# Weight sums for the output products: added by VectorE out of SBUF, and all weight sums begun earlier on a timer of their own

## The chip, the core and the metric

The kernel runs as one program on one NeuronCore of a Trainium2 chip. The metric is the device time of one execution in microseconds. A core has a matrix engine (TensorE, PE in the profile; its weight loads are PEld), a vector engine (VectorE, DVE), a scalar engine (ScalarE, ACT), a general engine (GpSimd, POOL) and a sync engine (SyncE, SP) whose queue issues most transfers. PE writes its results to PSUM; DVE and ACT take them from there to SBUF. All engines run at once and wait for each other through semaphores.

## The reference

Attention over four batches, eight heads, 768 positions of 64, in which each query sees the 31 nearest keys and 24 block summaries (the maximum over each block of 32 keys, the mean over each block of 32 values); then a gated network:

```python
def _moe_ref(x, w1, w2, w3, w_out):      # x: 3072 x 512, the heads side by side
    a = x @ w1                           # 512 x 1024
    b = x @ w2                           # 512 x 1024
    h = a * b @ w3                       # 1024 x 1024
    return (h @ w_out)                   # 1024 x 512
```

All inputs and outputs are float32. Since nothing stands between the last two products, the kernel multiplies `w3 @ w_out` once (1024 x 512) and uses that as the one output weight.

## The kernel before

**Products.** A float32 matrix is held as two halves of a narrower type, a high one and the rest ("low", `low` at L120), and a product takes three matmuls: high by high, low by high, high by low. Nearly every matmul of the network is 128 x 128 by 128 x 512. I count work in such matmuls and call one a *product* (512 columns; `U` in the code is 512, and the counter `given` counts columns handed to PE).

**Stages.** The 3072 tokens are six blocks of 512. PE's order is fixed by the program (a manual schedule for PE), as one stream (`products_in_order`, L973): 192 products that fold `w3 @ w_out` into the eight tiles `wp[0..7]` (each 128 x 2 x 512: high and low); then blocks 0 and 1 in the plain way (`gate`, `project`: 192 + 96 products for each block); then blocks 2+3 and blocks 4+5 in pairs (`gates`, `project_fast`) by a scheme with seven block products for eight (`NK = 7`), with 336 + 168 products for each pair. So the first pair begins at product 192 + 2 x 288 = 768. In between, `run` (L996) cuts the stream and the attention work of a pair of heads is put in (`two_steps`, L1282): scores (`sc`), softmax, transposes (`tp`), outputs (`po`).

**Weight sums.** The seven-product scheme needs sums of weight blocks. For the gates they are made per quarter q = 0..3 (`sums_of_gates`, L936), for the output weights per half c = 0, 1 (`sums_of_output`, L947). Both use `stationary` (L664), a generator. It loads four blocks `a11, a12, a21, a22` of 128 x 512 into a tile `wr`; four DVE instructions (L689, L691, L695, L700) make the four sums; for each sum `finished` makes a high half on ACT (L679) and a low half on DVE (L121) in a tile `sp`, and SP stores `sp` to DRAM (L685; `wS` for gates, `pS` for the output). The products load them again from there through `flow_in` (L712), at most six tiles `ws` ahead, and only sums whose store is in the set `stored`. Products that need no sum come from spilled weights (`spill_weights`, `spill_wp`).

For a gate quarter the load is four DVE additions of high and low halves out of SBUF (L942). For an output half it is a way through DRAM: `spill_high` (L927) stores the high half of each `wp[i]` into a tile `pR`; `join_wp` (L930) adds the low half onto it by an accumulating transfer that POOL issues; `load` (L949) then fetches four pieces of 256 KB into `wr` from SP, and waits nine steps.

**Pace.** The sums are a list `background` of generators, the moving operands of the pairs (`moving_x`, L766) a list `tasks`. `tend` (L981) takes one step of the first task, or, where no task can go on, one step of the first sum; `run` calls it every 4.5 products (`4.5 * U`), and whenever the stream cannot go on. The four gate sums enter the list in slot 64 of the first part (L1176), the output sums in the attention steps (8,1) and (9,0) (L1262). The slots from 47 to 66 share the stream evenly up to `TO_SLOTS` (437 products).

**Order on the queues.** PE is always in program order. SP is in program order in the first part (up to 437 products), POOL in the second. Elsewhere a planner orders ACT, DVE and SP: an instruction that comes earlier in the program goes first among those that the planner holds to be ready by its own cost estimates. On the chip each engine works its queue strictly in the planned order, so an instruction that waits holds everything behind it.

**Buffers.** Tag `x` has six buffers: the four `x` tiles of a plain block, the gate sums' `sp` tiles and all `ws` tiles. Tag `ring` has five (raw weights, pairs of `h`, gate sums' `wr`, later `hr`). Tag `wp` has eight (the `wp` tiles, later `tmp` and the output sums' `sp`). Tag `raw` has two (keys and values of later batches, the output sums' `wr`).

Of the kernel before, what the change touches and what calls it, by code (L numbers as in the profile page):

```python
# [11 lines left out]
F32 = mybir.dt.float32  # L12
# [4 lines left out]
ALU = mybir.AluOpType  # L17
# [3 lines left out]
P = 128  # L21
# [32 lines left out]
RING = 5  # L54
# [19 lines left out]
def attention_moe(ctx, tc, qG, kW, kT, vP, vW, vB, mask, w1, w2, w3T, wo, out, outT):  # L74
    nc = tc.nc
    B, NPAIR, _, S = kT.shape
    S -= PAD
    NB = S // BLOCK
    U = TOKENS
# [10 lines left out]
    NF = w1.shape[0] * FQ // P  # L90
    NJ = w3T.shape[2] // 2 // P
    DO = out.shape[1]
    NK = 7
# [19 lines left out]

    wS = [[tc.dram_tile([P, 2, KH * FQ], F32, name=f"wS{k}_{q}") for q in range(NQ)] for k in range(NK)]
    pS = {k: [tc.dram_tile([P, 2, 2 * DH], F32, name=f"pS{k}_{c}") for c in range(NF // 4)] for k in range(2, NK - 1)}
    pR = [tc.dram_tile([P, 2, 2, DO], F32, name=f"pR{c}") for c in range(NF // 4)]
    pW = [tc.dram_tile([P, 2, DO], F32, name=f"pW{i}") for i in range(NF)]
    vS = [tc.dram_tile([P, P], F32, name=f"vS{b}") for b in range(B)]

# [533 lines left out]
    def staggered(works):  # L653

        active = []
        while works or active:
            if works:
                active.append(works.pop(0))
            active = [work for work in active if next(work, 0)]
            yield 1  # L660

    stored = set()

    def stationary(name, load, to_dram, home, apart=False):  # L664


        if apart:
            two = [sb.tile([P, 2, 512], F32, name="wr", tag="raw", bufs=2) for _ in range(2)]
            t = [[two[i][:, j] for j in range(2)] for i in range(2)]
        else:  # L670
            whole = sb.tile([P, 2, 2, 512], F32, name="wr", tag="ring", bufs=RING)
            t = [[whole[:, i, j] for j in range(2)] for i in range(2)]
        yield from load(t)
        (a11, a12), (a21, a22) = t
        yield 1

        def finished(k, raw):
            to = sb.tile([P, 2, 512], F32R, name="sp", **home)
            nc.scalar.copy(to[:, 0], raw)  # L679
            yield 1  # L680
            low(nc.vector, to[:, 1], raw, to[:, 0])
            yield 1
            yield 1
            yield 1
            nc.sync.dma_start(to_dram(k), to.bitcast(F32))  # L685
            stored.add((name, k))

        works = []
        nc.vector.tensor_tensor(a22, a21, a22, ALU.add)  # L689
        yield 1  # L690
        nc.vector.tensor_tensor(a21, a11, a21, ALU.subtract)  # L691
        works.append(finished(2, a22))
        next(works[0])
        yield 1
        nc.vector.tensor_tensor(a11, a22, a11, ALU.subtract)  # L695
        works.append(finished(5, a21))
        next(works[0])
        next(works[1])
        yield 1
        nc.vector.tensor_tensor(a12, a12, a11, ALU.subtract)  # L700
        if apart:
            yield from staggered([*works, finished(4, a11), finished(3, a12)])
            return

        yield from staggered(works)
        for _ in range(3):
            yield 1
        yield from staggered([finished(4, a11), finished(3, a12)])

# [56 lines left out]
    def moving_x(n, at):  # L766

        o = ORDERS[n]
        k = o.ids[at]

        def start():
            while any(kept.get((n, half), 0) < NC for half in range(2 if k > 1 else 1)):
                yield -1
            t = sb.tile([P, 2, KH, U], F32R, name="xT", tag="w12", bufs=8)
            works = []
            for c in range(KH):
                b = [[raws[n, half][c + i * KH] if (n, half) in raws else None for half in range(2)] for i in range(2)]
                works.append(moving(o, k, b, (t[:, 0, c], t[:, 1, c]), o.before.get(k, (k,))))
            yield from staggered(works)
            xT[n, k] = t  # L780

        tasks.append(start())
# [141 lines left out]
        n = DO if i >= NF // 2 else DH  # L924
        nc.sync.dma_start(pW[i][:, :, :n], wp[i][:, :, :n].bitcast(F32))

    def spill_high(i):  # L927
        nc.sync.dma_start(pR[i % (NF // 2) // 2][:, i // (NF // 2), i % 2], wp[i][:, 0].bitcast(F32))

    def join_wp(i):  # L930


        to = pR[i % (NF // 2) // 2][:, i // (NF // 2), i % 2]
        nc.gpsimd.dma_start(to, wp[i][:, 1].bitcast(F32), accum_op=ALU.add)

    def sums_of_gates(q):  # L936

        def load(t):
            for j, w in enumerate(("w1", "w2")):
                hi, lo = (weights[w, q][:, i].rearrange("p (k c) f -> p k (c f)", k=2).bitcast(F32) for i in range(2))  # L940
                for c in range(2):
                    nc.vector.tensor_tensor(t[j][c], hi[:, c], lo[:, c], ALU.add)  # L942
                yield 1

        return stationary("w%d" % q, load, lambda k: wS[k][q], {"tag": "x", "bufs": 6})

    def sums_of_output(c):  # L947

        def load(t):  # L949
            for h in range(2):  # L950
                for i in range(2):
                    to = t[i][h].rearrange("p (j d) -> p j d", d=DH)
                    nc.sync.dma_start(to, pR[c][:, h, :, i * DH : (i + 1) * DH])
            yield from range(1, 10)

        return stationary("p%d" % c, load, lambda k: pS[k][c], {"tag": "wp", "bufs": NF}, True)

    def network():
        for u in range(2):
# [16 lines left out]
        yield from network()  # L976

    stream = products_in_order()
    given, tended = [0.0], [0.0]

    def tend():  # L981


        some = False
        for works in (tasks, background):
            while works:
                n = next(works[0], 0)
                if n > 0:
                    return True
                if n < 0:  # L990
                    break
                works.pop(0)
                some = True
        return some

    def run(columns):  # L996

        while given[0] < columns:
            n = next(stream, 0)
            if n <= 0:  # L1000
                if n == 0 or not tend():
                    return
                continue
            given[0] += n
            if given[0] >= tended[0]:
                tended[0] = max(tended[0] + 4.5 * U, given[0])
                tend()

    def place(s):
        return divmod(s, NPAIR)  # L1010
# [162 lines left out]
        66: [lambda: fetch_sums(6)],  # L1173
        67: [lambda: fetch_sums(7)],
    }
    WORK.setdefault(64, []).append(lambda: background.extend(sums_of_gates(q) for q in range(NQ)))  # L1176
    for q in range(NQ):
        WORK.setdefault(46 + 3 * q, []).append(lambda q=q: spill_weights(q))
    for i in range(NF):
        WORK.setdefault(48 + i, []).append(lambda i=i: spill_wp(i))  # L1180
    for i in range(NF):
        WORK.setdefault(58 + i, []).append(lambda i=i: spill_high(i))
    RATE = 8000
    LATER_RATE = 2744

# [65 lines left out]
    def begins(m):  # L1251
# [7 lines left out]
    EXTRA = {  # L1259
        (7, 0): [lambda: moving_x(1, 0), lambda: moving_x(1, 1)],  # L1260
        (8, 0): [lambda: gates_flow(1), lambda: flow_in(4), lambda: moving_x(1, 2)],
        (8, 1): [lambda: background.append(sums_of_output(0))],  # L1262
        (9, 0): [*(lambda k=k: moving_x(1, k) for k in range(3, NK)), lambda: background.append(sums_of_output(1))],
    }
    for i in range(NF):
        EXTRA.setdefault((4 + i // 4, i // 2 % 2), []).append(lambda i=i: join_wp(i))

    turned = {}

# [140 lines left out]
```

## Time and profile before

| | |
|---|---|
| median of 3 runs | 518.35 us (513.8 to 519.22) |
| the profiled execution | 515.73 us |
| its span, first to last instruction | 513.9 us |
| mean granted PE clock | 0.99 |
| matmuls of the network that take most: `ln` of the gates | 672, 155.3 us busy |
| output sums: first and last fetch of `pR` | 241.1 and 322.5 us |
| output sums: first and last store to `pS` | 312.5 and 344.8 us |
| first and last fetch of `pS` as `ws` | 352.9 and 488.5 us |

The profiled execution spends 515.73 - 513.9 = 1.83 us outside its span. PE's busy time is a union of overlapping matmuls, so the idle time of PE, and stretches in which the same matmuls take longer, are what can be gained or lost.

### The profile page before, as it was taken

The numbers are of one execution on the slowest core, as the hardware profiler recorded it, in microseconds if no ns is written. First come the engines' busy times: TensorE is split into PE (matmuls) and PEld (weight loads), VectorE is DVE, ScalarE is ACT, GpSimd is POOL, SyncE is SP. The second block draws the span as 40 slices with busy tenths as digits, with TensorE's granted clock in tenths as the row PEclk, the third lists the DMA queues.
The fourth block names the chain that finished last, engine by engine and source line by source line (L and its number), as shares of the span: only waits on it lengthen the run. The fifth ranks groups of instructions, "written<-read, shape, count | busy, mean of one in ns | idle before, by whom it ended". The sixth has DMA issues, their size and how long they took to land.

```text
span 513.9 us, 10576 instructions
## 1 busy us (share of the span) xinstructions
PE 484.7 (94%) x3804; PEld 395.2 (77%) x3804; DVE 363.5 (71%) x881; ACT 313.6 (61%) x874; POOL 92.6 (18%) x177
## 2 busy tenths in 40 slices
PE   0889999999998969999889999999999999999997
PEld 0667778888877858888678888878888888888886
DVE  5969886897768588697176597469999029229972
ACT  5489864775889569686399487853734421522710
POOL 1024522100435242335040402020000000000000
PEclk9999999999999979999989999999999999999999
DMA  8998698999799999899876698997669766556652
GB/s 346 412 408 264 228 352 280 370 399 411 245 296 265 318 270 289 274 293 318 277 203 220 206 347 298 329 300 245 206 190 282 230 198 204 186 185 204 208 187 98
DMA packets 53764, 139.29 MB, mean 271 GB/s; under 512 B 6224, under 2 KB 19280, under 8 KB 51152
## 3 DMA queue, kind: packets, MB, share of 16 engines
q1 hardware_dynamic: 45072, 111.78, 63.3%
q0 software_dynamic: 7488, 24.75, 16.9%
q10 hardware_dynamic: 1152, 2.10, 1.2%
q8 instruction: 30, 0.49, 0.4%
q14 instruction: 22, 0.18, 0.1%
HBM read 105.89 MB, written 32.70 MB: 270 GB/s over the span
## 4 chain that ended last, share of the span: by engine, by line
PE 71%; ACT 10%; DMA 9%; DVE 7%; issue 1%; SPq 1%; ACTq 0%; DVEq 0%
PE ln L740 42%; PE mm L125 21%; DMA wS<-sp 3%; DMA v<-vS 3%; PE po L457 3%; ACT sm L404 3%; PE sc L376 3%; DVE wf L206 2%; DVE w L121 2%; PE tp L434 2%; DMA wr<-pR 1%; ACT w L220 1%; ACT sm L414 1%; DVE wf L203 1%; DMA wraw<-in_wo_dram 1%
## 5 line engine op out<-in xcount | busy, mean ns | idle before, releaser
L740 PE MATMUL ln<-xT,ws 128*128 128x512 f32 x672 | 155.3, 391 | 1.0 <-DVE hr L760 1.0
L740 PEld LDWEIGHTS ln<-xT,ws 128*128 128x128 f32 x672 | 125.4, 188 | 28.3 <-DVE hr L760 1.4
L125 PE MATMUL mm<-x,w 128*128 128x512 f32 x384 | 90.6, 396 | 0.0
L125 PEld LDWEIGHTS mm<-x,w 128*128 128x128 f32 x384 | 72.8, 191 | 16.2 <-issue 0.5
L404 ACT ACTIVATE sm<-sm,mx 128x120 f32<-128x120 f32 x192 | 73.6, 390 | 9.0 <-DVE mx L390 9.0
L740 PE MATMUL ln<-hT,ws 128*128 128x512 f32 (+1 forms) x348 | 76.9, 382 | 0.0
L760 DVE TENSOR_TENSOR tmp<-ln,tmp 128x512 f32<-128x512 f32 (+1 forms) x53 | 35.8, 677 | 57.2 <-PE ln L740 43.0
L740 PEld LDWEIGHTS ln<-hT,ws 128*128 128x128 f32 x348 | 63.8, 188 | 12.7
L125 PE MATMUL mm<-w,w 128*128 128x512 f32 x192 | 50.0, 410 | 14.8 <-ACT w L220 12.2
L642 ACT CAST hT<-hr 128x512 fp32r<-128x512 f32 x56 | 32.2, 622 | 50.7 <-DVE hr L817 40.1
L125 PEld LDWEIGHTS mm<-w,w 128*128 128x128 f32 x192 | 36.0, 193 | 25.7 <-ACT w L220 12.9
L414 ACT ACTIVATE sm<-sm,mx 128x120 f32<-128x120 f32 x128 | 40.3, 388 | 10.5 <-DVE mx L410 6.4
L125 PE MATMUL mm<-wp,h 128*128 128x512 f32 x192 | 46.3, 395 | 0.0
L390 DVE CUSTOM_DVE_ANT_0 sm<-sc,mask_sb 128x120 f32<-128x120 f32 x192 | 40.7, 276 | 6.2 <-PE sc L376 6.2
L125 PEld LDWEIGHTS mm<-wp,h 128*128 128x128 f32 x192 | 35.4, 188 | 8.4 <-issue 0.5
L325 POOL DMA_DIRECT2D v<-in_vW_dram x48 | 25.3, 565 | 72.8 <-PE po L457 66.9
L121 DVE TENSOR_TENSOR hT<-hr,hT 128x512 fp32r<-128x512 f32 x56 | 35.5, 685 | 3.5 <-ACT hT L642 3.3
L404 ACT ACTIVATION_READ_ACCUMULATOR sm<-sm,mx 128x1 f32 x192 | 37.3, 194 | 0.0
L376 PE MATMUL sc<-k,q 64*64 64x120 f32 x768 | 26.6, 274 | 5.4 <-issue 3.9
L121 DVE TENSOR_TENSOR w<-wf,w 128x1024 fp32r<-128x1024 f32 (+1 forms) x22 | 25.6, 1166 | 8.2 <-ACT w L220 8.2
L220 ACT CAST w<-wf 128x1024 fp32r<-128x1024 f32 (+1 forms) x22 | 21.4, 973 | 14.8 <-DVE wf L206 13.4
L758 ACT COPY tmp<-ln 128x512 f32<-128x512 f32 x32 | 18.6, 586 | 16.8 <-PE ln L740 15.5
(74 smaller groups left out, 588.4 us busy)
## 6 DMA issues: line engine op xcount, KB each, us to landing
ws<-wS SPq DMA_DIRECT2D x56, 512.0 KB
wraw<-in_w3T_dram SPq DMA_DIRECT2D x8, 1024.0 KB
wraw<-in_w_dram SPq DMA_DIRECT2D x8, 1024.0 KB
wS<-sp SPq DMA_DIRECT2D x16, 512.0 KB
ws<-pS SPq DMA_DIRECT2D x16, 512.0 KB
wS<-w SPq DMA_DIRECT2D x12, 512.0 KB
ws<-pW SPq DMA_DIRECT2D x24, 256.0 KB
k<-in_kW_dram POOLq DMA_DIRECT2D x14, 368.0 KB, 8.4
```

Of the source, the lines that this page charges most:

```text
L121: eng.tensor_tensor(dst, src, hi.bitcast(F32), ALU.subtract)
L125: nc.tensor.matmul(acc, lhsT=a, rhs=b, start=first and i == 0, stop=last and i == len(terms) - 1)
L220: nc.scalar.copy(t[:, 0, some], f[:, some])
L325: (nc.gpsimd if u > 1 else nc.sync).dma_start(v[rows, g], vW[u, p, rows, g])
L376: nc.tensor.matmul(sc[h][64 * g : 64 * g + 64, i * KR : (i + 1) * KR], lhsT=q[rows, i * P + 64 * g : i * P + 64 * g + 64], rhs=k[rows, i, ...
L390: nc.vector.tensor_tensor_reduce(out=sm[:, j], in0=sc[h][:, i * KR : (i + 1) * KR], in1=mask_sb[:, 0 if blk == 0 else 2 if blk == BLOCKS - ...
L404: nc.scalar.activation(sm[:, j], sm[:, j], AF.Exp, bias=mx[:, 0, j : j + 1], scale=-1.0, accum_out=mx[:, 1, j : j + 1])
L414: nc.scalar.activation(sm[:, j], sm[:, j], AF.Copy, scale=mx[:, 2, j : j + 1])
L642: nc.scalar.copy(dst[0], src)
L740: nc.tensor.matmul(bank[:, cols], lhsT=x, rhs=y[:, cols], start=c + j == 0 and (split or k in o.first), stop=c == steps - 1 and j == 2 and ...
L758: nc.scalar.copy(parts[to][:, cols], got)
L760: nc.vector.tensor_tensor(parts[to][:, cols], got, parts[more][:, cols], ALU.add)
```

## The change

The way through DRAM is taken out: the tiles `pR`, `spill_high`, `join_wp` and their slots are gone. The load of an output sum becomes eight DVE additions of 128 x 256, straight from the high and low halves in `wp`, two to a step. Its `wr` now comes from tag `ring` and its `sp` tiles from tag `x`, as for the gates, and the `apart` variant is gone. All six sums enter the list in slot 58, gates first. Sums have a timer of their own (every 3.3 products) and no longer wait until no task can go on; the tasks keep the timer of 4.5. In every sum two more steps lie between the first two stores and the second two (5 for 3).

```diff
-    pR = [tc.dram_tile([P, 2, 2, DO], F32, name=f"pR{c}") for c in range(NF // 4)]
...
-    def stationary(name, load, to_dram, home, apart=False):
-        if apart:
-            two = [sb.tile([P, 2, 512], F32, name="wr", tag="raw", bufs=2) for _ in range(2)]
-            t = [[two[i][:, j] for j in range(2)] for i in range(2)]
-        else:
-            whole = sb.tile([P, 2, 2, 512], F32, name="wr", tag="ring", bufs=RING)
-            t = [[whole[:, i, j] for j in range(2)] for i in range(2)]
+    def stationary(name, load, to_dram, home):
+        whole = sb.tile([P, 2, 2, 512], F32, name="wr", tag="ring", bufs=RING)
+        t = [[whole[:, i, j] for j in range(2)] for i in range(2)]
...
-        if apart:
-            yield from staggered([*works, finished(4, a11), finished(3, a12)])
-            return
         yield from staggered(works)
-        for _ in range(3):
+        for _ in range(5):
             yield 1
         yield from staggered([finished(4, a11), finished(3, a12)])
...
-    def spill_high(i):
-        nc.sync.dma_start(pR[i % (NF // 2) // 2][:, i // (NF // 2), i % 2], wp[i][:, 0].bitcast(F32))
-    def join_wp(i):
-        to = pR[i % (NF // 2) // 2][:, i // (NF // 2), i % 2]
-        nc.gpsimd.dma_start(to, wp[i][:, 1].bitcast(F32), accum_op=ALU.add)
...
     def sums_of_output(c):
         def load(t):
             for h in range(2):
                 for i in range(2):
-                    to = t[i][h].rearrange("p (j d) -> p j d", d=DH)
-                    nc.sync.dma_start(to, pR[c][:, h, :, i * DH : (i + 1) * DH])
-            yield from range(1, 10)
-        return stationary("p%d" % c, load, lambda k: pS[k][c], {"tag": "wp", "bufs": NF}, True)
+                    for j in range(2):
+                        hi, lo = (wp[h * NF // 2 + 2 * c + j][:, w, i * DH : (i + 1) * DH].bitcast(F32) for w in range(2))
+                        nc.vector.tensor_tensor(t[i][h][:, j * DH : (j + 1) * DH], hi, lo, ALU.add)
+                    yield 1
+        return stationary("p%d" % c, load, lambda k: pS[k][c], {"tag": "x", "bufs": 6})
...
-    given, tended = [0.0], [0.0]
-    def tend():
+    given, tended, summed = [0.0], [0.0], [0.0]
+    SUMS_EVERY = 3.3 * U
+    def tend(lists=(tasks, background)):
...
-        for works in (tasks, background):
+        for works in lists:
...
                 tended[0] = max(tended[0] + 4.5 * U, given[0])
-                tend()
+                tend((tasks,))
+            if given[0] >= summed[0]:
+                summed[0] = max(summed[0] + SUMS_EVERY, given[0])
+                tend((background,))
...
-    WORK.setdefault(64, []).append(lambda: background.extend(sums_of_gates(q) for q in range(NQ)))
+    WORK.setdefault(58, []).append(lambda: background.extend([*(sums_of_gates(q) for q in range(NQ)), *(sums_of_output(c) for c in range(NF // 4))]))
...
-    for i in range(NF):
-        WORK.setdefault(58 + i, []).append(lambda i=i: spill_high(i))
...
-        (8, 1): [lambda: background.append(sums_of_output(0))],
-        (9, 0): [*(lambda k=k: moving_x(1, k) for k in range(3, NK)), lambda: background.append(sums_of_output(1))],
+        (9, 0): [lambda k=k: moving_x(1, k) for k in range(3, NK)],
     }
-    for i in range(NF):
-        EXTRA.setdefault((4 + i // 4, i // 2 % 2), []).append(lambda i=i: join_wp(i))
```

## The prediction

> **What bounds the kernel now.** I read the head of the page first, then who PE waited for, then the timeline around each of those waits.
>
> ```profile
> span 513.9 us, 10576 instructions
> PE 484.7 (94%) x3804; PEld 395.2 (77%) x3804; DVE 363.5 (71%) x881; ACT 313.6 (61%) x874; POOL 92.6 (18%) x177
> ```
> ```profile
> PE mm L125 <- ACT w L220: 12.2, 3, 11.4
> ```
>
> PE is busy for 94%, so a change in transfers can win only where PE stands or runs slowly. 513.9 - 484.7 = 29.2 us are idle; 11.4 of them are one wait at the start, which the change doesn't touch. The rest is in a few places. The largest that names this change is at 255 us (timelines of DVE, ACT and PE; columns: start, length, work, in brackets the idle time before and who ended it):
>
> ```profile
> 252.08 2.88 PE L740 MATMUL ln<-xT,ws 128*128 128x512 f32 x12
> ...
> 254.53 0.69 DVE L689 TENSOR_TENSOR wr<-wr 128x512 f32<-128x512 f32 x1 [11.39 <-DMA wr<-pR]
> ...
> 256.09 1.25 ACT L414 ACTIVATE sm<-sm,mx 128x120 f32<-128x120 f32 x4 [5.54 <-DVE mx L410]
> ...
> 257.87 3.45 PE L457 MATMUL po<-sm,v 120*64 120x64 f32 x64 [2.90 <-ACT sm L442]
> ...
> 263.14 1.04 PE L376 MATMUL sc<-k,q 64*64 64x120 f32 x30 [0.66 <-ACT xraw L477]
> ```
> ```profile
> 264.12 13.21 PE L740 MATMUL ln<-xT,ws 128*128 128x512 f32 x57
> ...
> 286.77 2.08 PE L457 MATMUL po<-sm,v 120*64 120x64 f32 x64
> ...
> 290.59 13.21 PE L740 MATMUL ln<-xT,ws 128*128 128x512 f32 x57
> ```
>
> Read upwards: DVE stood 11.39 us for the fetch of the output sum; behind it in DVE's queue was the reciprocal (L410), for which ACT stood 5.54 us, and behind ACT's normalizing the copy (L442) that PE needs. The same work, outputs and scores between two runs of `ln`, takes 290.59 - 286.77 = 3.82 us undisturbed, and here 264.12 - (252.08 + 2.88) = 9.16: **place B loses 5.34 us**. The idle time PE shows is only 2.90 + 0.66; the rest is clock (windows; columns: stretch, its length, PE busy, granted clock, DMA share, GB/s):
>
> ```profile
> 187.00:191.00 4.00, 3.77 (x35) 0.50 1.08 260
> ...
> 256.00:260.00 4.00, 2.13 (x40) 0.69 0.37 128
> 260.00:264.00 4.00, 3.34 (x94) 0.89 0.69 186
> ```
>
> The other places, each between the same kinds of work:
>
> ```profile
> 153.83 2.09 PE L457 MATMUL po<-sm,v 120*64 120x64 f32 x64
> ...
> 159.75 1.66 PE L125 MATMUL mm<-wp,h 128*128 128x512 f32 x6
> ...
> 179.01 1.15 PE L457 MATMUL po<-sm,v 120*64 120x64 f32 x32
> ...
> 189.03 12.84 PE L125 MATMUL mm<-x,w 128*128 128x512 f32 x48
> ...
> 235.64 11.17 PE L125 MATMUL mm<-wp,h 128*128 128x512 f32 x48
> ```
> ```profile
> 313.25 2.08 PE L457 MATMUL po<-sm,v 120*64 120x64 f32 x64
> ...
> 317.66 13.24 PE L740 MATMUL ln<-xT,ws 128*128 128x512 f32 x57
> ...
> 337.99 3.73 PE L740 MATMUL ln<-xT,ws 128*128 128x512 f32 x15 [0.98 <-DVE hr L760]
> ```
>
> **Place E** (154 to 160) loses 159.75 - 153.83 - 3.82 = 2.10. **Place A** (179 to 202) loses 189.03 - 179.01 - 3.82 = 6.20, and its 48 matmuls after that take 12.84 where 48 others take 11.17, so 7.87 in all (the clock of 0.50 above). **Place C** (313) loses 317.66 - 313.25 - 3.82 = 0.59. **Place D** (337) loses the 0.98 of its row. Together 16.9 us: what can be won at most.
>
> **The change, part by part.**
>
> *The way through DRAM goes.*
>
> ```profile
> DVE wr L689 <- DMA wr<-pR: 15.0, 2, 11.4
> ```
> ```profile
> pR<-wp SPq DMA_DIRECT2D x8, 256.0 KB
> pR<-wp POOLq DMA_DIRECT2D x8, 256.0 KB, 6.9
> ...
> wr<-pR SPq DMA_DIRECT2D x8, 256.0 KB
> ```
> ```profile
> POOL v L325 <- DMA pR<-wp: 0.9, 1, 0.9
> ```
>
> 24 transfers go, 8 from POOL and 16 from SP, and with them both waits of DVE (15.0 us in two): 11.4 at place B and the other 3.6 ahead of D, for which DVE is then late. The new sums wait for nothing outside SBUF: `wp` is written long before. So B wins 5.3 and D 1.0. What is late next at B: the half c = 1 is then in work there, and its casts on ACT; I take them as hidden (rival 1 prices it). At C, ACT's copy of `xraw` stood behind casts of output sums, which now come earlier: 0.6. On POOL the eight joins stood in program order among the fetches of q, k and v; one fetch waited 0.9 for a join.
>
> *Eight additions of 128 x 256 for each half.* Nearest row:
>
> ```profile
> L760 DVE TENSOR_TENSOR tmp<-ln,tmp 128x256 f32<-128x256 f32 x2 | 0.8, 424 | 1.8 <-PE ln L740 1.8
> ```
>
> 16 x 0.424 = 6.8 us on DVE. They go beside PE's work. Their place follows from the pace. A gate sum now has 22 steps (20 before), counted from the yields of `stationary`, an output sum 24. Slot 58 lies 8 of the 19 equal slots before 437 products: the slots are 35/3 = 11.7 products long, so it is at 343.7 (slot 64 was at 413.7). Gates: 22 x 3.3 = 72.6 products each, done at 343.7 + 4 x 72.6 = 634; outputs 24 x 3.3 = 79.2 each, at 713 and 793. Product 474 is at 159.75 and product 768 at 252.08, so 0.314 us each between them, and the output sums are in the program from about 210 to 258 us, not up to 345. There DVE has this room:
>
> ```profile
> 190.00:215.00 25.00, 25.00 (x242) 20.52 (x241) 19.75 (x60) 19.84 (x67) 8.00 (x16) 0.95 0.89 274
> 215.00:240.00 25.00, 25.00 (x248) 20.70 (x247) 21.61 (x79) 20.12 (x78) 9.14 (x20) 1.00 0.95 304
> ```
>
> DVE is busy 41.4 of 50 us, 8.6 idle, and the gate sums that lie in these windows before move ahead by 70 products, 22 us, so that most of one leaves them. Cost 0; if the cover is gone, up to 6.8 us.
>
> *All sums sooner, at 3.3.* What limits them is less the pace than the six `x` buffers, which are given out in program order:
>
> ```profile
> 123.94 0.69 DVE L689 TENSOR_TENSOR wr<-wr 128x512 f32<-128x512 f32 x1
> ...
> 134.69 0.56 ACT L482 CAST x<-po 128x512 fp32r<-128x512 f32 x1
> 135.26 0.61 ACT L679 CAST sp<-wr 128x512 fp32r<-128x512 f32 x1
> ```
>
> The first sum was ready at 124.6, its cast came at 135.26, right behind two `x` tiles that stand earlier in the program. Now the whole first gate sum stands ahead of those tiles (cast steps 4, 5, 16, 17: 357 to 400 products; the tiles at 402), and the second one ahead of the next two (474). From there to 672 products four buffers hold `x`, and all sums share two. A cast then waits until an earlier `sp` has been stored, and this wait is what makes place A:
>
> ```profile
> 162.38 8.01 DMA wS<-sp
> ...
> 171.79 9.22 DMA wS<-sp
> ```
> ```profile
> 178.59 0.62 ACT L679 CAST sp<-wr 128x512 fp32r<-128x512 f32 x1 [2.81 <-DMA wS<-sp]
> 181.09 0.62 ACT L679 CAST sp<-wr 128x512 fp32r<-128x512 f32 x1 [1.88 <-DMA wS<-sp]
> ```
>
> ACT stood 2.81 + 1.88 us and PE behind it. One turn of a buffer takes cast 0.62, low half 0.69 and store 8.01 to 9.22: 9.3 to 10.5 us. In the program the pairs of casts are now 12 and 10 steps apart, 39.6 and 33 products or 12.4 and 10.4 us; before, 10 and 10 steps of 4.5, 14.1 us. The two added steps keep most of that distance, and the rest stays just above a turn. The stores at A also lose company, since half of the eight joins were issued just ahead of them:
>
> ```profile
> 156.49 1.83 POOL L934 DMA_DIRECT2D pR<-wp x2 [0.29 <-issue]
> ...
> 163.67 0.88 POOL L934 DMA_DIRECT2D pR<-wp x1 [1.24 <-issue]
> ```
>
> So I take half of A as won, 4.0 of 7.9. Bounds: all of it, 7.9, where the stores are quicker or the casts later; nothing, or one more place like A (-7.9), where the casts still come before their buffers. Between these ends the half is nearest to the rows, since the wait is 4.7 us of a turn of 10 and the transfers that made the turn long partly go.
>
> *DVE's bursts at E.* There the additions of the second gate sum stood ahead of DVE's low half of `x`, for which PE waited. The sums now come 20 us sooner into a stretch (114 to 142 us) in which PE never stood. I take one more collision of the size of E, -2.1; the bounds are +2.1 (E goes too) and -4.2 (two).
>
> *SP in its fixed part.* Eight stores of `pR` go; four stores of the first gate sum take their place, at steps 8, 10, 20, 21 (370 to 413 products), behind them the fetches of slots 63 to 65. If the low halves are late, these fetches are. They have until 142 us; cost 0, and 0.9 (the one wait of PE for `v` in this class of fetch) if that isn't enough. The tasks' own timer isn't held up by sums, nor were tasks before: cost 0.
>
> **Sum.** 5.3 + 1.0 + 0.6 + 4.0 - 2.1 = 8.8 us. The profiled execution, 515.73 us (1.83 outside the span), would take 506.9. It stands 2.62 below the median of the three runs, 518.35; against that the forecast is 518.35 - 8.8 = 509.5 us.
>
> *A rule on the clock, weighed.* At B the clock fell to 0.69 after a gap of 2.90 us, and I priced B with the clock in it. The Trainium skill, "TensorE: Matmul & The Clock Gate", Part 1, says that the clock falls to half after an idle window of about 3.4 us and asks only that gaps stay below some 3 us. By that rule B would cost 2.90 + 0.66 = 3.56, and the sum would be 7.0, so 511.3 us. The trace doesn't agree, since its gaps are all shorter and the rows show 0.69 and 0.50; the measurement decides.
>
> **Rivals.**
>
> 1. *B stays, with another cause.* The second output half's casts need `x` buffers which `ws` tiles hold from 702 products on (`flow_in` runs up to six ahead), and each is free only when PE has used it. ACT would stand there instead of DVE. For: the fetches of two tiles every 24 products now share with these casts. Against: at 4.5 the fourth gate sum lay beside `ws` tiles too, and among PE's waits there is none for `ws`. Time: 518.35 - (8.8 - 5.3) = 514.9.
> 2. *A moves, it doesn't shrink.* In the two-buffer stretch (474 to 672) lie five pairs of casts, two each of gate sums 3 and 4 and the first of output half 0, at 10.4 to 12.4 us for a turn of up to 10.5. If A keeps its 7.9 and no collision of E's kind comes, the sum is 6.9 - 2.1 + 2.1 = 6.9, still faster; with one more wait of A's size it is 6.9 - 7.9 = -1.0, and the time 519.4: no change.
> 3. *Slower: A three times.* The same mechanism with two more waits of that size out of the five: 6.9 - 15.8 = -8.9, so 527.3. From 518.35 + 5.2 on it counts as slower, which needs 6.9 + 5.2 = 12.1 us of new waits, one and a half of A's size. For: the margin is between 0 and 3 us. Against: where the transfers were fewer, a pair of the third sum hardly waited:
>
> ```profile
> 205.89 0.62 ACT L679 CAST sp<-wr 128x512 fp32r<-128x512 f32 x1 [0.59 <-DMA wS<-sp]
> ```
>
> 4. *The sums aren't sooner*, as `ring` buffers are lacking (four hold `h`). B and D go even then, since no transfer is waited for: 518.35 - 6.9 = 511.5.
>
> **How the numbers follow.** A measurement of this kernel can tell about 1%, 5.2 us: faster is below 513.2, slower above 523.5. Forecast with its spread (A won between nothing and all, E's kind between -4.2 and +2.1, or rival 4): 0.64. Rival 1: 0.12. Rival 2: 0.13. Rival 3: 0.11. So faster 0.64, same 0.12 + 0.13 = 0.25, slower 0.11. The range goes down to all five places, 518.35 - 16.9 = 501.5, and up to 518, which takes in rival 1 and leaves out most of 2 and all of 3, about 2 in 10.
>
> **What would show it.** B right: no row of `wr` fetched, DVE's wait of 11.39 gone, outputs and scores near 255 us in about 3.8 us at clock 1.00. D right: no gap before `ln` at 337. A: ACT's total wait of `sp` for `wS<-sp` below the 4.7 us of its two rows, and 48 matmuls near 190 in 11.2 us. E's kind: a gap of PE between 114 and 160 released by DVE. The forecast is wrong if ACT waits for `sp` buffers for more than 7 us in total, if PE waits for `ws`, or if DVE's busy time rises by much more than 6.8.

## The result and the profile after

The changed kernel takes 520.15 us (median of 20 runs, 515.55 to 526.76), the kernel before, run beside it, 516.38 (20 runs, 513.8 to 522.79): a ratio of 1.0061, 95% interval 1.0035 to 1.0088. So it is a little slower, by less than the 1% that counts here. The forecast was 509.5 with a range of 501.5 to 518: the time lies outside it, and the gain of 8.8 us did not come.

The profiled execution took 519.39 us, 3.66 more than the one of before. In the changed file the lines have moved: L673 is the cast of `sp` on ACT (L679 before), L679 its store, L935 the new addition out of SBUF, L456 `po`, L375 `sc`, L476 the copy of `xraw`, L730 `ln`, L124 `mm`. The head of the page after, and lines of its view of waits (who waited <- for what: total us, count, longest):

```profile
span 517.6 us, 10541 instructions
PE 482.9 (93%) x3804; PEld 392.9 (76%) x3804; DVE 368.7 (71%) x897; ACT 314.3 (61%) x874; POOL 87.1 (17%) x169
```
```profile
ACT sp L673 <- DMA pS<-sp: 9.8, 3, 7.7
...
ACT sp L673 <- DMA wS<-sp: 6.9, 4, 3.6
```

PE is busy for 1.8 us less than before, and the span is 3.7 longer: PE stands more. DVE's waits for `pR` (15.0 us) are gone. ACT's waits for stores that hold buffers of `sp` are now 9.8 + 6.9 = 16.7 us; before they were 7.1, all for `wS`. The places where PE stood before, in PE's timeline after:

```profile
157.39 2.09 PE L456 MATMUL po<-sm,v 120*64 120x64 f32 x64
...
163.66 1.66 PE L124 MATMUL mm<-wp,h 128*128 128x512 f32 x6
...
179.51 5.73 PE L124 MATMUL mm<-x,w 128*128 128x512 f32 x24 [1.96 <-ACT g L524]
185.17 2.09 PE L456 MATMUL po<-sm,v 120*64 120x64 f32 x64
...
189.68 11.17 PE L124 MATMUL mm<-x,w 128*128 128x512 f32 x48
...
262.57 2.88 PE L730 MATMUL ln<-xT,ws 128*128 128x512 f32 x12
...
269.33 13.22 PE L730 MATMUL ln<-xT,ws 128*128 128x512 f32 x57
```

Between `po` and the next network matmul A now takes 189.68 - 185.17 = 4.51 (10.02 before), B 269.33 - (262.57 + 2.88) = 3.88 (9.16 before); undisturbed it is 3.82. E stays: 163.66 - 157.39 = 6.27 (5.92 before). Two places are new: **F** at 211 and **G** at 237. The same stretches before, and then after:

```profile
209.27 2.08 PE L457 MATMUL po<-sm,v 120*64 120x64 f32 x64
...
213.22 10.52 PE L125 MATMUL mm<-x,w 128*128 128x512 f32 x45
...
231.82 2.08 PE L457 MATMUL po<-sm,v 120*64 120x64 f32 x64
```
```profile
208.26 2.08 PE L456 MATMUL po<-sm,v 120*64 120x64 f32 x64
...
212.94 0.39 PE L375 MATMUL sc<-k,q 64*64 64x120 f32 x2 [1.62 <-issue]
214.87 1.04 PE L375 MATMUL sc<-k,q 64*64 64x120 f32 x30 [1.54 <-ACT xraw L476]
215.85 10.49 PE L124 MATMUL mm<-x,w 128*128 128x512 f32 x45
...
234.42 2.09 PE L456 MATMUL po<-sm,v 120*64 120x64 f32 x64
...
240.69 0.63 PE L375 MATMUL sc<-k,q 64*64 64x120 f32 x2 [3.20 <-issue]
243.34 1.87 PE L375 MATMUL sc<-k,q 64*64 64x120 f32 x30 [2.02 <-ACT xraw L476]
245.14 12.16 PE L124 MATMUL mm<-wp,h 128*128 128x512 f32 x48
```

F went from 213.22 - 209.27 = 3.95 to 215.85 - 208.26 = 7.59, G from 235.64 - 231.82 = 3.82 to 245.14 - 234.42 = 10.72, and the 48 matmuls behind G from 11.17 to 12.16. All places together, by the time from one mark of PE to the next:

| stretch | forecast | after less before, us |
|---|---|---|
| start to the scores at 130 us (one gap at 90 us) | 0 | +2.3 |
| from there to E (one gap of 1.23 at 144) | +2.1 | +1.3 |
| E | 0 | +0.4 |
| between E and A (gap of 1.96 at 179) | 0 | +2.2 |
| A, with its 48 matmuls | -4.0 | -7.2 |
| F | 0 | +3.6 |
| G, with its 48 matmuls | 0 | +7.9 |
| B | -5.3 | -5.3 |
| between B and C | 0 | +0.4 |
| C | -0.6 | -0.6 |
| D | -1.0 | -1.0 |
| what is left | | -0.3 |
| sum (spans: 517.6 - 513.9) | -8.8 | +3.7 |

The gap at 90 us stands behind a fetch of raw weights (`wraw`) that came late: ACT waited 4.31 us for it, 1.97 before; up to there the engines' queues hold the same work in the same order in both kernels. It is there in six of the ten profiles of kernels made from the changed one, with 0.2 to 2.1 us, and in none of the four of kernels made from the one before. Whether the change has a part in it stays open, and I don't count it to the change; without this row the two profiled executions differ by 1.4 us and not by 3.7.

What PE waits for at F and G is found by reading ACT and DVE there, upwards from ACT's copy of `xraw`, which frees the outputs' PSUM for the scores. DVE, ACT and SP after (start, length, work, idle time before and who ended it):

```profile
209.34 1.76 DVE L935 TENSOR_TENSOR wr<-wp 128x256 f32<-128x256 f32 x5
211.02 0.68 DVE L530 TENSOR_TENSOR g<-mm,g 128x512 f32<-128x512 f32 x1
```
```profile
211.74 0.62 ACT L531 CAST h<-g 128x512 fp32r<-128x512 f32 x1 [2.55 <-DVE g L530]
212.26 0.58 ACT L476 COPY xraw<-po 128x512 f32<-128x512 f32 x1
...
239.49 0.62 ACT L673 CAST sp<-wr 128x512 fp32r<-128x512 f32 x1 [7.72 <-DMA pS<-sp]
240.01 0.58 ACT L476 COPY xraw<-po 128x512 f32<-128x512 f32 x1
242.18 0.62 ACT L673 CAST sp<-wr 128x512 fp32r<-128x512 f32 x1 [1.59 <-DMA pS<-sp]
242.70 0.58 ACT L476 COPY xraw<-po 128x512 f32<-128x512 f32 x1
```
```profile
225.01 5.24 SPq L775 DMA_DIRECT2D ws<-wS  x4
230.69 0.81 SPq L679 DMA_DIRECT2D pS<-sp  x2
```

At F five additions of output half 0 stand in DVE's queue ahead of the gate's product `g` (L530); ACT's cast of `h` waits for that, and behind the cast stand the copies of `xraw`, with a cast of half 0 between them. The first copy (212.26) is late by the additions, with no cast of half 0 ahead of it; the second (214.24) by them and by that cast. At G ACT stands 7.72 us with the cast of half 1, until a store of half 0 has read its buffer (half 1's own sum was ready at about 237, so without the store ACT would still have stood some 5 us); behind that cast stands the first copy of `xraw`, behind the next cast (1.59 us) the second. The two stores that they wait for were issued only at 230.69, behind four fetches of `ws` of 512 KB that SP sent first, though the second of the two `sp` tiles was finished at 229.0. In the chain of waits of the same execution the second store takes 10.97 us, up to the second of these casts:

```profile
231.11 10.97 DMA pS<-sp
```

### The profile page after: what moved, and what is told of

Its sections match the earlier page's. It is cut to its first block, busy times and chain, and to the rows that moved or that the text cites. A ratio compares the mean times of both kernels' runs of the same rounds, so it can differ in the third digit from the quotient of the medians.

```text
span 517.6 us, 10541 instructions
## 1 busy us (share of the span) xinstructions
PE 482.9 (93%) x3804; PEld 392.9 (76%) x3804; DVE 368.7 (71%) x897; ACT 314.3 (61%) x874; POOL 87.1 (17%) x169
## 4 chain that ended last, share of the span: by engine, by line
PE 53%; DVE 17%; ACT 15%; DMA 11%; issue 2%; SPq 0%; POOL 0%; ACTq 0%; DVEq 0%; POOLq 0%
PE ln L730 41%; PE mm L124 7%; ACT sm L403 6%; DMA pS<-sp 3%; DMA wS<-sp 3%; PE po L456 3%; DVE wf L205 2%; DVE w L120 2%; ACT sm L413 2%; ACT w L219 2%; DMA wraw<-in_w_dram 2%; DMA v<-vS 2%; PE sc L375 1%; DVE wr L923 1%; DVE sp L120 1%
## 5 line engine op out<-in xcount | busy, mean ns | idle before, releaser
L730 PE MATMUL ln<-xT,ws 128*128 128x512 f32 x672 | 155.2, 391 | 0.1
L730 PEld LDWEIGHTS ln<-xT,ws 128*128 128x128 f32 x672 | 125.4, 188 | 27.3 <-DVE hr L750 0.5
L124 PE MATMUL mm<-x,w 128*128 128x512 f32 x384 | 89.5, 392 | 3.9 <-ACT g L524 2.0
L124 PEld LDWEIGHTS mm<-x,w 128*128 128x128 f32 x384 | 71.4, 188 | 20.2 <-ACT g L524 2.4
L730 PE MATMUL ln<-hT,ws 128*128 128x512 f32 (+1 forms) x348 | 76.9, 382 | 0.0
L730 PEld LDWEIGHTS ln<-hT,ws 128*128 128x128 f32 x348 | 63.7, 188 | 12.7
L124 PE MATMUL mm<-w,w 128*128 128x512 f32 x192 | 50.0, 410 | 14.9 <-ACT w L219 12.3
L124 PEld LDWEIGHTS mm<-w,w 128*128 128x128 f32 x192 | 36.0, 193 | 25.8 <-ACT w L219 13.0
L124 PE MATMUL mm<-wp,h 128*128 128x512 f32 x192 | 47.4, 401 | 1.2 <-ACT o L553 1.2
L124 PEld LDWEIGHTS mm<-wp,h 128*128 128x128 f32 x192 | 36.2, 192 | 10.0 <-ACT o L553 1.7
L375 PE MATMUL sc<-k,q 64*64 64x120 f32 x768 | 26.8, 274 | 10.5 <-issue 6.5
L120 DVE TENSOR_TENSOR sp<-wr,sp 128x512 fp32r<-128x512 f32 x24 | 16.4, 689 | 23.8 <-ACT sp L673 23.8
L375 PEld LDWEIGHTS sc<-k,q 64*64 64x64 f32 x768 | 21.5, 136 | 14.2 <-issue 8.2
```

The lines of the kernel that those rows point to most:

```text
L120: eng.tensor_tensor(dst, src, hi.bitcast(F32), ALU.subtract)
L124: nc.tensor.matmul(acc, lhsT=a, rhs=b, start=first and i == 0, stop=last and i == len(terms) - 1)
L375: nc.tensor.matmul(sc[h][64 * g : 64 * g + 64, i * KR : (i + 1) * KR], lhsT=q[rows, i * P + 64 * g : i * P + 64 * g + 64], rhs=k[rows, i, ...
L730: nc.tensor.matmul(bank[:, cols], lhsT=x, rhs=y[:, cols], start=c + j == 0 and (split or k in o.first), stop=c == steps - 1 and j == 2 and ...
```

## The experiments

Theory 1: the output sums, put right behind the gate sums, come into a stretch where nothing covers them. Rival: the way through DRAM was no bottleneck, or the gate sums' earlier start is what costs. Kernels that ran side by side are compared by their medians, others by their ratios to the kernel before, which ran beside each group (medians 516.53, 517.21 and 516.86).

**The change in halves.** `sbuf_only` is the kernel before with the additions out of SBUF in the place of `pR`; homes, slots and timer stay:

```diff
...
-                    to = t[i][h].rearrange("p (j d) -> p j d", d=DH)
-                    nc.sync.dma_start(to, pR[c][:, h, :, i * DH : (i + 1) * DH])
-            yield from range(1, 10)
+                    for j in range(2):
+                        hi, lo = (wp[h * NF // 2 + 2 * c + j][:, w, i * DH : (i + 1) * DH].bitcast(F32) for w in range(2))
+                        nc.vector.tensor_tensor(t[i][h][:, j * DH : (j + 1) * DH], hi, lo, ALU.add)
+                    yield 1
...
```

> Output sums are added by DVE out of SBUF, but begin where they began before, on the shared timer of 4.5, in the tags raw and wp; the gate sums are as before. Buffer theory (what the whole change lost, it lost by ACT standing for sp buffers in tag x): this part alone never puts an output sum into tag x, so places B, C and D go (5.3 + 0.6 + 1.0), A and E stay, and the time is 516.4 - 6.9 = 509.5 us; ACT's wait of sp for pS stores is 0. DVE theory (the sixteen additions, 6.8 us of DVE, cost what the change lost): no gain, 514 to 520 us.

`sooner_only` keeps the way through DRAM and takes the rest: gates from slot 58, a timer of 3.3, five steps.

```diff
-        for _ in range(3):
+        for _ in range(5):
...
+            if given[0] >= summed[0]:
+                summed[0] = max(summed[0] + SUMS_EVERY, given[0])
+                tend((background,))
...
-    WORK.setdefault(64, []).append(lambda: background.extend(sums_of_gates(q) for q in range(NQ)))
+    WORK.setdefault(58, []).append(lambda: background.extend(sums_of_gates(q) for q in range(NQ)))
```

> The way of the output sums through DRAM stays, and they begin where they began before; gate sums begin in slot 58, all sums have their own timer of 3.3, five steps lie between the stores. Buffer theory: the gate sums come sooner but in the same two buffers, so A goes to other places near 177 and 211 us and about keeps its size, while B stays (5.3): 515 to 519 us, ACT's wait of sp for wS stores 6 to 10 us. DVE theory: the additions that are missing here are what cost, and the time is below before by what A gave up, 509 to 512 us.

`sbuf_only` took 509.28 (ratio 0.9846, 0.9804 to 0.9888), `sooner_only` 519.88 (1.0056, 1.0032 to 1.008), a little above what was expected of it. PE's timeline of `sbuf_only` at A, and at C:

```profile
179.13 2.08 PE L456 MATMUL po<-sm,v 120*64 120x64 f32 x64
...
185.00 11.20 PE L124 MATMUL mm<-x,w 128*128 128x512 f32 x48
...
303.23 2.08 PE L456 MATMUL po<-sm,v 120*64 120x64 f32 x64
...
311.66 13.87 PE L739 MATMUL ln<-xT,ws 128*128 128x512 f32 x57
```

The time is the expected one, the places are not. A was to stay and shrank to 5.87, its 48 matmuls to 11.20, with the gate sums where they were: there the transfers that left were enough. C was to go and grew from 4.41 to 311.66 - 303.23 = 8.43, since ACT waits there for stores of `pS`, a wait that was to be 0. B went (3.88). In `sooner_only` A shrank as well (191.25 - 185.48 = 5.77), so either half does it; but E grew from 5.92 to 9.06, and B stayed, with DVE's wait for `pR`:

```profile
254.89 0.69 DVE L689 TENSOR_TENSOR wr<-wr 128x512 f32<-128x512 f32 x1 [10.51 <-DMA wr<-pR]
```

The second half's fetch of `pR` makes a stop of its own there, at 289, where PE lost nothing before: DVE waits 3.97 us for it, PE 3.17, and outputs and scores take 294.78 - 287.13 = 7.65.

```profile
293.37 1.48 PE L376 MATMUL sc<-k,q 64*64 64x120 f32 x32 [3.17 <-issue]
```

So the removal of the way through DRAM gains 7.3 us alone by the medians (5.8 to 10.1 by the interval of the ratio). The sooner start gains nothing while that way is still there; part of what it lost is this new stop, so the run doesn't say what the start is worth by itself.

**The place of the output sums.** `output_later` is the changed kernel with the output sums entering the list where they did before:

```diff
-    WORK.setdefault(58, []).append(lambda: background.extend([*(sums_of_gates(q) for q in range(NQ)), *(sums_of_output(c) for c in range(NF // 4))]))
+    WORK.setdefault(58, []).append(lambda: background.extend(sums_of_gates(q) for q in range(NQ)))
...
-        (9, 0): [lambda k=k: moving_x(1, k) for k in range(3, NK)],
+        (8, 1): [lambda: background.append(sums_of_output(0))],
+        (9, 0): [*(lambda k=k: moving_x(1, k) for k in range(3, NK)), lambda: background.append(sums_of_output(1))],
```

> The changed kernel, but the output sums enter the list where they did before, in (8,1) and (9,0), and not in slot 58. Buffer theory: output half 0 leaves the stretch with two free buffers, so the stop of PE near 237 us (3.20 + 2.02 idle, clock lowered) goes and ACT's wait for pS stores falls below 3 us; but now all eight tiles sp of the output lie beside ws tiles, so at most that stop is won: 511 to 516 us. DVE theory: the same additions at another time, 518 to 522 us.

`second_half_later` does that with half 1 alone; half 0 stays in the list of slot 58.

> The changed kernel, but of the output sums only half 0 follows the gates from slot 58; half 1 enters the list in (9,0) as before. Store theory (near 237 us the casts of half 1 stand for the stores of half 0, which leave while four ws tiles are fetched, and PE stands 5.2 us and runs at a lowered clock): that place goes, the one at 211 (3.2 us, half 0's additions in DVE's queue ahead of the gate's product) stays; 520.2 - 7 = 513 us, ACT's wait for pS stores from 9.8 to below 3. Total-load theory (any earlier output sum costs through DVE's load): half of the 12.0 us between the changed kernel and output_later, 514 us, and the place at 237 is only smaller, not gone.

`output_later` took 508.13 (0.9835, 0.9804 to 0.9865), better than expected, though its interval overlaps that of `sbuf_only`; `second_half_later` 513.4 (0.9924, 0.9894 to 0.9955). From 1.0061 the one ratio step is 0.0137, half 1, and the next 0.0089, half 0: 7.1 and 4.6 us of 516.4. PE's timeline of `output_later` at F, then of `second_half_later` at F:

```profile
208.42 2.08 PE L456 MATMUL po<-sm,v 120*64 120x64 f32 x64
...
213.08 10.50 PE L124 MATMUL mm<-x,w 128*128 128x512 f32 x45
```
```profile
208.31 2.08 PE L456 MATMUL po<-sm,v 120*64 120x64 f32 x64
...
212.71 0.39 PE L375 MATMUL sc<-k,q 64*64 64x120 f32 x2 [1.33 <-issue]
214.69 1.87 PE L375 MATMUL sc<-k,q 64*64 64x120 f32 x30 [1.60 <-ACT xraw L476]
216.50 12.30 PE L124 MATMUL mm<-x,w 128*128 128x512 f32 x45
```

Without half 1, G is 3.81, gone and not only smaller, and ACT never waits for `pS`. Without half 0 as well, F is 213.08 - 208.42 = 4.66. The places follow the sums.

**Place, or buffers?** `more_buffers` gives two of the four `sp` tiles of each gate sum a home in tag `wf`, which I took for idle there; `later_buffers` is `output_later` with this edit, `sbuf_more_buffers` is `sbuf_only` with it.

```diff
-            to = sb.tile([P, 2, 512], F32R, name="sp", **home)
+            to = sb.tile([P, 2, 512], F32R, name="sp", **(home if k in (2, 5) or name[0] == "p" else {"tag": "wf", "bufs": 6}))
```

> The changed kernel, but the gate sums' tiles of products 4 and 3 come from tag wf, of which two of six buffers are idle at that time, so that the sums have four buffers and not two. Buffer theory: ACT's wait of sp for stores falls from 16.7 us to below 8 (the output sums' 9.8 partly stay), and the time falls by 2 to 8 us against the changed kernel, to 512 to 518 us. DVE theory: no change, 518 to 522 us.

> output_later with tiles of products 4 and 3 of the gate sums in tag wf, so that the gate sums have four buffers. Buffer theory: the gap of PE near 179 (1.9 us, behind 3.9 us of ACT for a wS store) goes and ACT's wait of sp for wS stores falls from 6.4 to below 2.5; 508.1 - 2 = 506 us, as more_buffers stood 2.0 below the changed kernel. Rival: ACT's wait there is cover, and PE stops for something else: 508 to 510.

> sbuf_only with the same other buffers. sbuf_only shows what is left of place A as 0.74 + 0.70 us of PE near 183 and 0.61 near 207, and ACT's wait of sp for wS stores as 4.6 us. Buffer theory: these go, 509.3 - 2.5 = 506.8 us. Rival: 509 to 511, as the sums run up earlier against something else.

`more_buffers` took 518.13 (1.0026, 0.9999 to 1.0053): ACT's wait for `wS` fell from 6.9 to 1.7, the one for `pS` stayed (10.5), so that both together are 12.2 and not below 8. The time lies on the border between the two theories. The other two missed both of theirs: 513.9 (0.995, 0.9923 to 0.9977), 1.2% above `output_later`, and 528.74 (1.0222, 1.017 to 1.0274). The view of waits of `later_buffers`, then of `sbuf_more_buffers`:

```profile
DVE sm L389 <- DMA wS<-sp: 4.9, 1, 4.9
```
```profile
DVE sm L389 <- DMA wS<-sp: 4.8, 3, 2.5
```

The tag wasn't idle: softmax tiles `sm` live in it and now wait for the stores. The wait moved from ACT to DVE; where the 19 us of `sbuf_more_buffers` above `sbuf_only` come from is not traced. So these runs don't say what free buffers would give.

**G and F one at a time.** `flow_later` is the changed kernel with the fetches that filled the `x` buffers ahead of G one attention step later:

```diff
-        (8, 0): [lambda: gates_flow(1), lambda: flow_in(4), lambda: moving_x(1, 2)],
+        (8, 0): [lambda: gates_flow(1), lambda: moving_x(1, 2)],
+        (8, 1): [lambda: flow_in(4)],
```

> The changed kernel, but the first four ws tiles are given out and fetched in (8,1) and not in (8,0), about 40 products later, so that four of the six x buffers are free while half 1 is in work; all sums stay where the change put them. Buffer theory of the place at 237: ACT's wait of sp for pS stores falls from 9.8 us to below 3, PE's 3.20 + 2.02 there go; 520.2 - 6 = 514 us, as second_half_later. If fetches of ws come too late for product 768, PE shows a wait for ws. Rival (DVE is what stops there): no change, 519 to 521 us.

`half0_on_pool` is `second_half_later` with the additions of half 0 on POOL instead of DVE (`nc.vector if c else nc.gpsimd`).

> second_half_later (513.4 us), but the eight additions of output half 0 are made by POOL and not by DVE; nothing else is changed. Queue theory (at 209 five of these additions, 1.76 us, stand in DVE's queue ahead of the gate's product, ACT waits 2.55 us for that, and its copies of xraw, for which PE waits, come late): the 2.93 us of PE at 211 to 215 shrink to below 1.2 and the clock there stays at 1.00; 513.4 - 4 = 509 us. Cast theory (what is late is ACT's cast of half 0 between the two copies, which stands for its buffer and its sum): the gap keeps more than 2 us; 512 to 514 us.

`pace_45` is the changed kernel with `SUMS_EVERY = 4.5 * U`, so that every sum comes later, the gates' as well.

> The changed kernel with a timer of 4.5 products for the sums in place of 3.3. Gates end at 343.7 + 4 x 22 x 4.5 = 740 products, output half 0 at 848, half 1 at 956, so both halves lie behind the stretch with two buffers, as in output_later, though nothing but the pace is changed. Position theory (what costs is that output sums lie between 634 and 768 products): within 3 us of output_later's 508.1, so 506 to 512. Own-timer theory (what costs is that sums no longer wait for the tasks): 516 to 520.

`flow_later` took 513.97 (0.9952, 0.9921 to 0.9983), the time that was expected. PE's timeline at G, and its waits:

```profile
234.82 2.08 PE L456 MATMUL po<-sm,v 120*64 120x64 f32 x64
...
240.29 8.00 PE L124 MATMUL mm<-wp,h 128*128 128x512 f32 x34
```
```profile
ACT sp L673 <- DMA wS<-sp: 9.0, 6, 3.9
ACT sp L673 <- DMA pS<-sp: 3.8, 1, 3.8
```

G fell from 10.72 to 5.47 and the wait for `pS` from 9.8 to 3.8: the `ws` tiles and their fetches ahead of the stores made the greater part of G. (Below 3 was expected for the wait. What is left, 1.65 above the 3.82, is another one: ACT waits 5.11 us there for half 1's own sum on DVE. The execution profiled was the slowest of its twelve, 519.31, and the wait for `wS` rose from 6.9 to 9.0, so only G is read from it.) In `half0_on_pool` the product `g` followed at once, at 208.32 where it stood at 211.02, and F fell to 212.30 - 207.39 = 4.91. But DVE was not relieved: while POOL made its additions, one instruction of DVE, the low half of `xT`, took 6.29 us where its neighbour took 0.69. The pooled keys that DVE makes came later, POOL's copies of them began at 237.48 (235.99 in `second_half_later`), and PE, 4.3 us earlier than there, waited for them (POOL, DVE, then PE):

```profile
212.12 5.59 POOL L935 TENSOR_TENSOR wr<-wp 128x256 f32<-128x256 f32 x8
```
```profile
211.96 6.29 DVE L120 TENSOR_TENSOR xT<-xraw,xT 128x512 fp32r<-128x512 f32 x1 [0.44 <-ACT xT L641]
```
```profile
239.11 3.48 PE L375 MATMUL sc<-k,q 64*64 64x120 f32 x64 [4.15 <-POOL k L362]
```

Its times scatter from 505.66 to 516.31 (six runs, median 514.67), so its worth isn't settled. Nor does it part the two theories: the sums came later on POOL, and with them half 0's casts left F, the first to 225.91 from 213.54 in `second_half_later`. That the additions are the greater part is read from the rows at F: the first copy of `xraw` was late with no cast of half 0 ahead of it. `pace_45` took 512.06 (0.9902, 0.987 to 0.9935): the sums in the same list and order, only later, and 1.6% of the time goes. That is just outside the 506 to 512 of the position theory, and far from the 516 to 520 of the other; but the gate sums came later too, and ACT's wait for `wS` fell from 6.9 to 2.8, so not all of the 1.6% need be the output sums'.

**What the rest of the change is worth.** Two edits on top of `output_later`: gates from slot 64 as before (`later_slot64`), and three steps between the stores as before (`later_three`).

> output_later (508.1 us), but the gate sums begin in slot 64 as before, not 58. Of the change this leaves the additions out of SBUF, the sums' own timer and the two steps. Sooner-helps theory: 509.5 to 511 us, with place A back near 183. Sooner-is-neutral theory: within 1.5 us of output_later.

> output_later with three steps between the first two stores and the second two, and not five. Turn theory: the pairs of casts come 10 and 10 steps of 3.3 apart, 10.4 us at a turn of 9.3 to 10.5, so ACT's wait of sp for wS stores rises from 6.4 us to 8 or more; 509 to 512 us. Rival (the planner places the casts by their buffers and not by the steps): no difference, 507 to 509 us.

513.13 (0.9908, 0.9883 to 0.9934) and 515.96 (0.997, 0.9938 to 1.0002): both worse than `output_later`, by 0.7% and 1.4%, more than expected. In `later_three` ACT's wait for `wS` fell from 6.4 to 4.8, against the theory that without the two added steps the casts come before their buffers are free; PE instead waited 3.05 us for `ws` at 307, and its stretch at 188 was 7.62 for 4.51. In `later_slot64` A did not come back (4.51), but F did: 215.24 - 206.52 = 8.72 for 4.66, though no output sum lies there. It is a gate sum this time: three of its additions, 1.89 us from 207.58 on, stand in DVE's queue ahead of `g`, and ACT's cast of `h` waits 2.68 us. So F belongs to the place and not to the output sums as such. Each such edit makes the planner order everything behind it anew. By the ratios `later_slot64` loses some 4 us, about what F lost (4.1), and `later_three` some 7; what the 7 are made of stays open.

## Why the prediction was wrong, by its own steps

**The way through DRAM goes: right.** B -5.3, C -0.6 and D -1.0 are the forecast to a tenth, no row fetches `pR`, and outputs and scores at B take 3.88 us. The removal alone gave 509.28, by chance the time that was forecast for all of the change: A gave more than its half, C lost where it was to gain, and no collision of E's kind came.

**A as half won (4.0): right in sign, too small by itself.** A and its 48 matmuls gave 7.2; 2.2 of it came back just ahead, where ACT now waits 3.62 + 1.79 us for `wS` and PE 1.96 behind it. Net 5.0. The prediction gave the credit to fewer joins and a longer distance together. `sbuf_only` and `sooner_only` show that each half of the change was enough for A, but not in the same way: without the joins ACT's wait for `wS` fell from 7.1 to 4.6 us, and with the sooner start it rose to 8.0 and lay elsewhere. In the changed kernel it is 6.9 and not below the 4.7 named as A's sign: there the wait hardly shrank. It moved, as in rival 2, but to a place where PE loses less.

**One more collision of E's kind (2.1): near in size, by another engine.** 1.3 up to E and 0.4 at E. The sign was to be a gap released by DVE; the new gap, 1.23 us at 144, is released by ACT's copy of `o` (L553), and ACT had cast two tiles of a gate sum (139.29 and 140.19) before it. So the size was in part luck.

**Eight additions, cost 0: the first step that failed.** DVE's load was right (16 additions in 5.9 us; 6.8 were forecast), but the argument was from DVE's idle time over 25 us, and what counted was the order: 1.76 us ahead of `g`, with a cast of half 0 behind, came to 3.6 at F in the changed kernel. In `second_half_later` they came to 4.2 more than before's 3.95, and 1.8 in the 45 matmuls behind. The cover was there on the average and not at that place.

```profile
L935 DVE TENSOR_TENSOR wr<-wp 128x256 f32<-128x256 f32 x16 | 5.9, 418 | 0.0
```

**All sums sooner: the step that failed most.** This part of the prediction asked for the turn of a buffer among gate sums in the stretch of 474 to 672 products, and left the output sums, placed at 713 to 793 products by its own count, at 0. There `ws` tiles hold four of the six `x` buffers; half 1's casts had only half 0's buffers left, and the stores that free these were late on SP. G lost 7.9 us; with the `ws` tiles later (`flow_later`) `po` to the next matmul there took 5.25 us less. Rival 1 had this cause, `ws` tiles in half 1's `x` buffers, with ACT standing; but it looked for it at B, released by PE's use of `ws`, in B's place and not beside a B that was won. Rival 2 had the time, 519.4, with one more wait of A's size; the place was another. Rivals 3 and 4 did not come. What the prediction had written as the sign that would make it wrong, ACT waiting over 7 us for `sp` buffers, was there with 16.7; but before the change it was 7.1 already, so that the sign could not tell much.

In ratios: without the path 0.9846; the rest of the change on top, with the output sums in their old place, 0.9835; half 0 moved, 0.9924; half 1 too, 1.0061. The first two don't differ by more than their intervals. What the change gains it gives back by one line, the place of the output sums in the list.

**The clock.** The price of a gap was again above its length: 7.9 us for 3.20 + 2.02 idle at G. A window of the changed kernel within these gaps, one of it around the gaps of 1.62 + 1.54 at F, then one of `second_half_later` behind 1.33 + 1.60 at F (columns: stretch, its length, busy time and count of PE, PEld, DVE, ACT and POOL, granted clock, DMA share, GB/s):

```profile
240.00:244.00 4.00, 1.29 (x16) 0.95 (x20) 3.67 (x6) 2.21 (x5) 0.68 (x2) 0.55 1.05 276
```
```profile
212.00:216.00 4.00, 1.51 (x33) 1.16 (x34) 3.95 (x8) 3.70 (x7) 0.88 (x2) 1.00 0.98 312
```
```profile
215.00:220.00 5.00, 5.00 (x38) 4.00 (x31) 5.00 (x35) 4.55 (x20) 0.00 (x0) 0.50 0.85 259
```

So the changed kernel's gaps at F, about as long as those of `second_half_later`, left the clock at 1.00, and it stayed there from 215 to 220. The Trainium skill, "TensorE: Matmul & The Clock Gate", Part 1, has the clock halve after an idle window of about 3.4 us that runs freely, without regard to the work. The half agrees with 0.50, and a window that runs freely fits that like gaps once cost the clock and once didn't; that gaps shorter than the window are safe, these rows don't bear out.

## What to carry to other kernels

Price moved work at the place it moves to: read there what stands behind it in each in-order queue and who holds the buffers it needs; an engine's idle share over a stretch says neither. When a change both removes a transfer and moves work, run the removal alone and the move alone, since here the removal gained 7.3 us and the place of two sums took it all back. Before a buffer is borrowed, look up who else takes from its tag.

## What the hardware showed that was not expected

A pause of PE in two parts, 1.33 + 1.60 us with scores between, was enough for a clock of 0.50 over the next 5 us; a pause in two parts of 1.62 + 1.54 in another run cost none. An addition of 128 x 256 out of SBUF took 5.59 us for eight on POOL, 0.70 each, and on DVE 1.76 for five in a row, 0.35 each, while the mean of the 16 is 0.418: those in a row overlap. While POOL worked on its eight (212.12 to 217.71 us of `half0_on_pool`), a DVE operation on two tiles of 128 x 512 in SBUF took 6.29 us (211.96 to 218.25); the same operation just before took 0.69. In this one place the work that was moved from DVE to POOL held DVE up for longer than it would have taken there.
